# A chained attention, SwiGLU and bilinear kernel on one core: the second product in six groups of 768 tokens with streamed left factors

## The chip, the cores and the metric

One Trainium2 chip, one of its cores. The time is the device time of one execution in microseconds; the figure of a kernel is the median of its runs. The engines are TensorE (PE in the profile, its weight loads PEld), VectorE (DVE), ScalarE (ACT), GpSimd (POOL) and SyncE (SP), which issues most DMA transfers.

## What is computed

```python
p_packed = sm_attn(p, k, v)               # 8 batches, 8 heads, 576 tokens, 64 wide, 32 packed rows
out = sm_attn(q, p_packed, p_packed)
x = out.transpose(0, 2, 1, 3).reshape(4608, 512)
h = x @ w_in;  x = (h * sigmoid(h)) @ w_out          # 512 -> 2048 -> 512
a = x @ w1;    b = x @ w2                            # 512 -> 1024, twice
result = ((a * b) @ w3) @ w_out2                     # 1024 -> 1024 -> 512
```

All values are float32. The kernel holds each factor of a matrix product as a high and a low part and adds three products (high x high, low x high, high x low).

## The kernel before

The kernel has two stages. The first does the attention and the SwiGLU block ("first product": tiles `ps_h` and `ps_x`, matmuls of 288 columns) and writes its result x transposed to DRAM (`x2_d`), half a batch at a time, from a tile `xs`. The second ("second product") computes `a`, `b`, `a * b` and the output; `w3 @ w_out2` has been multiplied beforehand into `w34`.

The second product goes over 9 groups of 512 tokens and, in each, over 4 pairs `mp` of 128-wide blocks of the 1024 inner columns: 36 items, each one call of `emit_ab`. An item multiplies 2x2 blocks with seven products where eight would be needed (Winograd's form). Its left factors (seven per pair, made of `w1`, x = 0, and of `w2`, x = 1, at line 941) lie split in SBUF tiles `w`; its right factors are seven combinations of four quarters of the group's x (`x2r`), made by `right_factors` on VectorE (sums) and on ScalarE and VectorE (high and low part) into tiles `xcb..` and `xct..`. The seven products are matmuls of 256 columns (`product`, line 1236, here "y matmuls"); both x lie side by side in one of four PSUM banks `b1` to `b4`, 12 matmuls to a product. ScalarE and VectorE combine the banks (`p1`, `p5`, `r1`, `r2`; the copies at line 82, the additions at line 1257), VectorE multiplies a by b (`gate`, line 1260) and splits the result (`abh`, `abl`, lines 82 and 91). `emit_o` multiplies that by `w34`: 24 matmuls of 512 columns (lines 98 to 100, tile `ps_o`), added up over the four items of a group in four PSUM banks, which `evict` then copies and stores.

The left factors of pairs 0 and 1 come split from DRAM (`w12_d`, two loads of 1792 KB each); those of pairs 2 and 3 are made during the first two items by `last_left_factors` (sums on VectorE, high part on ScalarE, low part on GpSimd, line 91) straight into the tile `w12_23`. After that all left factors stay in SBUF.

The program is written as one order of instructions; a scheduler lays out each engine's queue at compile time by a model of times: of the instructions that it takes to be ready, the earliest in the program goes first. On the chip each queue then runs strictly in that order. Tiles of a pool opened later lie where earlier tiles lay, and wait until those are given up.

## Time and profile before

| | before |
|---|---|
| runs: median (lowest to highest) | 1437.81 us (1437.04 to 1439.02), 3 runs |
| profiled execution, span from first to last instruction | 1436.1 us |
| TensorE, VectorE, ScalarE, GpSimd busy | 97%, 63%, 47%, 42% |
| first y matmul of the second product | 862.2 us |
| last matmul | 1432.0 us |

A row of the profile names the line, the engine, the operation, the tile written and the tiles read, the shape, and how many. TensorE's durations overlap, since matmuls are pipelined: a spacing is taken from starts. A figure in square brackets is the idle time of the engine before the instruction and what ended it.

### The profile page before, as it was taken

How to read it: one execution, taken by the hardware profiler on the slowest of the kernel's cores; microseconds unless marked ns; L12 is line 12 of the kernel's file. 1: busy time of each engine (PE TensorE's matmuls, PEld its weight loads, DVE VectorE, ACT ScalarE, POOL GpSimd, SP SyncE). 2: the span in 40 equal slices, each digit the busy share in tenths (PEclk: the TensorE clock that was granted, in tenths of full speed). 3: DMA queues.
4: the chain of work that ended last, by engine and by line, in shares of the span. 5: the costliest groups of instructions: out<-in, count | busy, mean ns of one | idle time of the engine just before them, and what ended most of it. 6: DMA issues, size and time to landing. Idle time of an engine off the chain costs nothing.

```text
span 1436.1 us, 25890 instructions
## 1 busy us (share of the span) xinstructions
PE 1390.7 (97%) x9548; PEld 1308.4 (91%) x9548; DVE 901.6 (63%) x1687; ACT 672.2 (47%) x1474; POOL 605.5 (42%) x626
## 2 busy tenths in 40 slices
PE   7799899999999999999999999999999999999998
PEld 5578899899999999999998998999999999999998
DVE  5897756558766488666578855635454553645453
ACT  6866556655666555664556544323232231322221
POOL 2778755856779657687567534100000000000000
PEclk9999899999999999999999999999999999999999
DMA  8697544844568343563557667011010110101000
GB/s 319 198 308 253 163 150 142 265 152 146 170 184 249 123 155 121 170 190 116 178 162 252 204 228 298 23 38 46 15 60 1 60 29 31 59 2 60 1 30 30
DMA packets 135967, 193.07 MB, mean 134 GB/s; under 512 B 14496, under 2 KB 92576, under 8 KB 135328
## 3 DMA queue, kind: packets, MB, share of 16 engines
q1 hardware_dynamic: 125344, 178.82, 39.1%
q10 hardware_dynamic: 10496, 12.59, 2.5%
q8 instruction: 75, 1.23, 0.4%
q14 instruction: 52, 0.43, 0.1%
HBM read 132.38 MB, written 58.98 MB: 133 GB/s over the span
## 4 chain that ended last, share of the span: by engine, by line
PE 70%; DVE 9%; DMA 7%; issue 4%; POOL 4%; ACT 4%; SPq 2%; ACTq 0%; DVEq 0%; POOLq 0%
PE ps_ab L1236 24%; PE ps_x L100 6%; PE ps_x L98 6%; PE ps_x L99 6%; PE ps_o L98 5%; PE ps_o L99 5%; PE ps_o L100 5%; PE ps_h L98 3%; PE ps_h L100 3%; PE ps_h L99 3%; SPq L115 2%; DMA mr<-m_d 1%; DMA m_d<-ms 1%; POOL z L189 1%; DVE sbd L251 1%
## 5 line engine op out<-in xcount | busy, mean ns | idle before, releaser
L98 PE MATMUL ps_x<-gh,wo 128*128 128x288 f32 x1024 | 301.9, 298 | 2.7 <-ACT gh L82 1.2
L99 PE MATMUL ps_x<-gh,wo 128*128 128x288 f32 x1024 | 301.0, 296 | 0.0
L100 PE MATMUL ps_x<-gl,wo 128*128 128x288 f32 x1024 | 289.1, 297 | 1.9 <-POOL gl L91 1.6
L91 POOL TENSOR_TENSOR gl<-gg,gh 128x288 fp32r<-128x288 f32 x256 | 227.9, 893 | 101.5 <-ACT gh L82 82.5
L1236 PE MATMUL ps_ab<-xct,w 128*128 128x256 f32 x1728 | 223.0, 284 | 1.7 <-DVE r L1257 1.4
L1236 PEld LDWEIGHTS ps_ab<-xct,w 128*128 128x128 f32 x1728 | 215.6, 190 | 3.0 <-DVE r L1257 1.6
L98 PEld LDWEIGHTS ps_x<-gh,wo 128*128 128x128 f32 x1024 | 193.0, 189 | 6.1 <-DVE xs L883 2.0
L99 PEld LDWEIGHTS ps_x<-gh,wo 128*128 128x128 f32 x1024 | 193.2, 189 | 2.1 <-issue 1.2
L100 PEld LDWEIGHTS ps_x<-gl,wo 128*128 128x128 f32 x1024 | 188.1, 189 | 4.3 <-POOL gl L91 3.6
L82 ACT ACTIVATE gh<-gg 128x288 fp32r<-128x288 f32 x256 | 112.8, 443 | 165.8 <-DVE gg L846 158.2
L91 POOL TENSOR_TENSOR mq<-mr,mq 128x256 fp32r<-128x256 f32 x168 | 136.7, 814 | 109.0 <-DVE mq L86 54.4
L846 DVE SCALAR_TENSOR_TENSOR gg<-sg,ps_h 128x288 f32<-128x288 f32 x256 | 114.6, 448 | 107.3 <-ACT sg L841 55.3
L1236 PE MATMUL ps_ab<-xcb,w 128*128 128x256 f32 x1296 | 177.5, 283 | 0.7 <-ACT w L82 0.4
L98 PE MATMUL ps_h<-a,mq 128*128 128x288 f32 x512 | 155.9, 305 | 18.0 <-DVE gg L846 13.8
L1236 PEld LDWEIGHTS ps_ab<-xcb,w 128*128 128x128 f32 x1296 | 168.1, 189 | 5.6 <-ACT w L82 0.6
L1257 DVE TENSOR_TENSOR r<-p,ps_ab 128x512 f32<-128x512 f32 x72 | 49.2, 683 | 184.3 <-PE ps_ab L1236 184.1
L99 PE MATMUL ps_h<-a,mq 128*128 128x288 f32 x512 | 152.4, 298 | 0.0
L100 PE MATMUL ps_h<-a,mq 128*128 128x288 f32 x512 | 151.9, 297 | 0.0
L841 ACT ACTIVATE sg<-ps_h 128x288 f32<-128x288 f32 x256 | 103.4, 404 | 82.3 <-PE ps_h L100 48.6
L98 PEld LDWEIGHTS ps_h<-a,mq 128*128 128x128 f32 x512 | 96.7, 189 | 25.9 <-DVE gg L846 19.0
L82 ACT ACTIVATE p<-ps_ab 128x512 f32<-128x512 f32 x72 | 43.1, 598 | 146.2 <-PE ps_ab L1236 139.8
L100 PE MATMUL ps_o<-w,abh 128*128 128x512 f32 x280 | 109.5, 391 | 0.0
(172 smaller groups left out, 2645.3 us busy)
## 6 DMA issues: line engine op xcount, KB each, us to landing
mr<-m_d SPq DMA_DIRECT2D x144, 128.0 KB, 2.6
raw<-in_moe_w_dram SPq DMA_DIRECT2D x32, 512.0 KB, 4.4
wz<-wi_d SPq DMA_DIRECT2D x48, 256.0 KB, 3.8
m_d<-ms SPq DMA_DIRECT2D x96, 128.0 KB, 3.0
x_d<-xs SPq DMA_DIRECT2D x20, 576.0 KB, 3.4
raw<-in_moe_w_out_dram SPq DMA_DIRECT2D x22, 512.0 KB, 4.3
out_dram<-ob SPq DMA_DIRECT2D x36, 256.0 KB, 2.0
vr<-in_v_dram SPq DMA_DIRECT2D x14, 640.0 KB, 4.1
```

What stands on the lines that cost most here:

```text
L82: A.activation(out=dst, in_=src, func=ACTF.Copy, scale=mul)
L91: (eng or V).tensor_tensor(out=lo, in0=src, in1=hi.bitcast(F32), op=ALU.subtract)
L98: T.matmul(out=dst, lhsT=wh, rhs=xh, start=start, stop=False)
L99: T.matmul(out=dst, lhsT=wl, rhs=xh, start=False, stop=False)
L100: return T.matmul(out=dst, lhsT=wh, rhs=xl, start=False, stop=stop)
L115: return eng.dma_start(out=out, in_=in_)
L189: G.tensor_tensor(out=z, in0=z, in1=word(I32, 0), op=ALU.add)
L251: (act_copy if plain else V.tensor_copy)(dst[r, 0, :, r], src[r])
L841: ins = A.activation(out=sg, in_=ps, func=ACTF.Tanh, scale=0.5)
L846: ins = V.scalar_tensor_tensor(out=gg, in0=sg, scalar=1.0, in1=ps, op0=ALU.add, op1=ALU.mult)
L1236: T.matmul(out=bank[:, x], lhsT=w[:, wp], rhs=xt[:, kt, xp], start=first and (x, kt, n) == (0, 0, 0), stop=last and (x, kt, n) == (1, 1, 2 ...
L1257: V.tensor_tensor(out=dst, in0=p, in1=q, op=op)
```

## The change

The second product goes over 6 groups of 768 tokens. A quarter of the group's x is 384 columns wide, and the y matmuls have 384 columns. An item runs the seven products for x = 0 (`w1`) and then for x = 1 (`w2`), 6 matmuls to a product; the gates of both blocks are spread over the second half. The left factors are streamed: `load_unit` brings those of one pair and one x (1792 KB) into one of four buffers, as often as there are half-items, 48 times. Those of pairs 2 and 3 are now stored to `w12_d` when they are made, in the first items, and loaded again. Output sums go over one item in PSUM and over the four items of a group in SBUF tiles `oacc`, by a copy on ScalarE in the first item and an addition on VectorE in the others. For all groups but the first, the sums of the right factors are made on GpSimd (`right_sums`), and four of the seven low parts too. `load_x2` of the next group is queued behind the last store of `xs`. The order of the products and of `emit_o` within an item is as before.

```diff
-    w12_d = dram.tile([128, 2, 2, 2, 7, 2, 128], F32, name="w12_d")
+    w12_d = dram.tile([128, KM2 // 2, 2, 2, 7, 2, 128], F32, name="w12_d")
...
-            move(out=x2_d[b, f], in_=xs)
+            behind["xs"] = move(out=x2_d[b, f], in_=xs).ins
...
-                    store(out=w12_d[:, :, x, kt, j], in_=t, age=0)
+                    store(out=w12_d[:, 0:2, x, kt, j], in_=t, age=0)
...
-    NG = NT // 512
-    x2r, x2c, w12, w34 = {}, {}, {}, {}
+    W = 384
+    GT = 2 * W
+    NG = NT // GT
+    MP = KM2 // 2
+    assert NG * GT == NT
+    x2r, x2c, w34 = {}, {}, {}
+    RIGHT = ("b11", "t1", "t2", "t4", "b21", "t3", "b22")
+    LEFT = {name: j for j, name in enumerate(("a11", "a12", "a22", "s1", "s2", "s3", "s4"))}
...
+    def quarters(g):
+        return [x2r[g][:, 2 * i:2 * i + 2, W * j:W * j + W] for i in range(2) for j in range(2)]
+    def temp(pool, tag, bufs):
+        return pool.tile([128, 2, W], F32, tag=tag, name=tag, bufs=bufs)
+    def right_part(g, name, src, eng=None):
+        c = early.tile([128, 2, 2, W], F32R, tag=f"xc{name}", name=f"xc{name}")
+        split(c[:, :, 0], c[:, :, 1], src, eng=eng)
+        x2c[g][name] = c
...
+    def first_right_factors():
+        b11, b12, b21, b22 = quarters(0)
+        t = temp(early, "xt", 1)
+        x2c[0] = {}
+        minus(t, b12, b11)
+        minus(b12, b22, b12)
+        right_part(0, "b11", b11)
+        yield
+        right_part(0, "t1", t)
...
+    def right_sums(g):
+        b11, b12, b21, b22 = quarters(g)
+        t1, t2, t4 = temp(early, "xt", 1), temp(mid, "tmp", 2), temp(mid, "tmp", 2)
+        minus(t1, b12, b11, G)
+        yield
+        minus(b12, b22, b12, G)
+        yield
+        minus(t2, b22, t1, G)
+        yield
+        minus(t4, t2, b21, G)
+        sums_of[g] = dict(b11=b11, t1=t1, t2=t2, t4=t4, b21=b21, t3=b12, b22=b22)
     def right_factors(g):
-        r = x2r.pop(g)
-        b11, b12, b21, b22 = (r[:, 2 * i:2 * i + 2, 256 * j:256 * j + 256] for i in range(2) for j in range(2))
-        t = early.tile([128, 2, 256], F32, tag="xt", name="xt")
         x2c[g] = {}
...
-        part("b11", b11)
-        yield
-        part("t1", t)
...
+        for n, name in enumerate(RIGHT):
+            right_part(g, name, sums_of[g][name], V if n % 2 else G)
+            yield
+    wunits, came2 = [], []
+    def load_unit():
+        n = len(came2)
+        mp, x = divmod(n % (2 * MP), 2)
+        t = wunits[n % len(wunits)]
+        move(out=t, in_=w12_d[:, mp, x])
+        came2.append(t)
+    def room_unit(pool):
+        wunits.append(pool.tile([128, 2, 7, 2, 128], F32R, name=f"unit{len(wunits)}"))
...
     def last_left_factors():
+        def load(n):
+            t = low.tile([128, 2, 512], F32, tag="zl", name="zl", bufs=2)
+            for y in range(2):
+                move(out=t[:, y], in_=late_d[2 * n + y])
+            return [t[:, y] for y in range(2)]
+        z = load(0)
         for n in range(4):
             x, kt = divmod(n, 2)
-            sums = early.tile([128, 4, 256], F32, tag="sums", name="sums")
+            sums = low.tile([128, 4, 256], F32, tag="suml", name="suml")
             def part(j, src):
-                t = w12[2, 3][:, :, x, kt, j]
+                t = low.tile([128, 2, 2, 128], F32R, tag="w12s", name="w12s", bufs=7)
                 split(t[:, :, 0], t[:, :, 1], src.rearrange("p (j n) -> p j n", j=2), eng=G)
-            for step in left_factors([z12h.pop((n, y)) for y in range(2)], sums, part):
+                move(out=w12_d[:, 2:4, x, kt, j], in_=t)
+            nz = load(n + 1) if n < 3 else None
+            for step in left_factors(z, sums, part):
                 step()
+                left_steps[0] += 1
                 yield
-            if n < 2:
-                load_z12(n + 2)
+            z = nz
...
-            room_second(0, early)
-            load_second(0)
-            for n in range(2):
-                load_z12(n)
-            drain(right_factors(0))
+            for _ in range(2):
+                room_unit(early)
+                load_unit()
+            load_w34(early, 0)
+            drain(first_right_factors())
...
+    for _ in range(2):
+        room_unit(top)
+        load_unit()
     for mp in range(1, MP):
-        room_second(mp, wb, top if mp == 1 else None)
-    for mp in range(1, MP):
-        load_second(mp)
+        load_w34(mid, mp)
...
-    def product(bank, mp, g, left, right, first, last):
+    def product(bank, w, g, left, right, first, last):
         xt = x2c[g][right]
-        for x in range(2):
-            for kt in range(2):
-                w = w12[mp][:, x, kt, LEFT[left]]
-                for n, (wp, xp) in enumerate(((0, 0), (1, 0), (0, 1))):
-                    T.matmul(
-                        out=bank[:, x], lhsT=w[:, wp], rhs=xt[:, kt, xp],
-                        start=first and (x, kt, n) == (0, 0, 0), stop=last and (x, kt, n) == (1, 1, 2),
-                        skip_group_check=True,
-                    )
-    last_left = last_left_factors()
+        for kt in range(2):
+            for n, (wp, xp) in enumerate(((0, 0), (1, 0), (0, 1))):
+                T.matmul(
+                    out=bank, lhsT=w[:, kt, LEFT[left], wp], rhs=xt[:, kt, xp],
+                    start=first and (kt, n) == (0, 0), stop=last and (kt, n) == (1, 2),
+                    skip_group_check=True,
+                )
...
+        gated = {}
+        def gate(m, t):
+            r = [gated[x, m][:, t] for x in range(2)]
+            V.tensor_tensor(out=r[0], in0=r[0], in1=r[1], op=ALU.mult)
+            split(*(a[:, t * W:t * W + W] for a in abt[g, m]), r[0])
+        for x in range(2):
+            wt = came2[2 * i + x]
+            nxt = side[0]
+            if x and mp == MP - 1 and g + 1 < NG:
+                nxt = right_factors(g + 1)
+            steps = 3 if i < 2 else 1
+            def step():
+                for _ in range(steps):
+                    next(nxt, None)
+            b1, b2, b3, b4 = (ps_ab.tile([128, 512], F32, tag=f"ab{j}", name=f"ps_ab{j}")[:, 0:W] for j in range(4))
+            r1, r2 = room(f"r{x}0"), room(f"r{x}1")
+            gated[x, m1], gated[x, m2] = r1, r2
+            p1, p5 = (low.tile([128, W], F32, tag=f"p{j}", name=f"p{j}") for j in (1, 5))
+            product(b1, wt, g, "a11", "b11", True, False)
+            act_copy(p1, b1)
+            step()
+            product(b3, wt, g, "s1", "t1", True, False)
+            act_copy(p5, b3)
+            step()
+            product(b2, wt, g, "s2", "t2", True, False)
+            add(r1[:, 1], p1, b2)
+            step()
+            product(b4, wt, g, "a22", "t4", True, True)
+            step()
+            if i and not x and not final:
+                emit_o(i - 1)
+            product(b1, wt, g, "a12", "b21", False, True)
+            act_copy(r1[:, 0], b1)
+            if x:
+                room_ab()
+                gate(m1, 0)
+            step()
+            product(b2, wt, g, "s3", "t3", False, True)
+            add(r2[:, 1], p1, b2)
+            add(r2[:, 0], r2[:, 1], b4, ALU.subtract)
+            add(r2[:, 1], r2[:, 1], p5)
+            if x:
+                gate(m2, 0)
+            step()
+            product(b3, wt, g, "s4", "b22", False, True)
+            add(r1[:, 1], r1[:, 1], b3)
+            if x:
+                gate(m1, 1)
+                gate(m2, 1)
+            step()
+            while len(came2) < min(2 * len(items2), 2 * i + x + 1 + len(wunits)):
+                if left_steps[0] < {4: 22, 5: 44}.get(len(came2), 0):
+                    break
+                load_unit()
...
     def emit_o(i):
         g, mp = items2[i]
-        if mp == 0:
-            oacc[g] = [ps_o.tile([128, DM], F32, tag="o", name="ps_o") for _ in range(4)]
-        for m in reversed(pair(mp)):
-            h_, l_ = abt.pop((g, m))
-            for t in range(4):
-                ts = slice(128 * t, 128 * t + 128)
-                mm3(
-                    oacc[g][t], h_[:, ts], l_[:, ts], w34[m][:, 0], w34[m][:, 1],
-                    m == pair(0)[1], m == pair(MP - 1)[0],
-                )
-    def evict(i, t0):
-        g, mp = items2[i]
-        if mp < MP - 1:
-            return
-        for t in (t0, t0 + 1):
-            if i + 1 < len(items2):
-                ob = wb.tile([128, DM], F32, tag="ob", name="ob", bufs=2)
+        ab = {m: abt.pop((g, m)) for m in pair(mp)}
+        for t in range(GT // 128):
+            ts = slice(128 * t, 128 * t + 128)
+            ps = ps_o.tile([128, DM], F32, tag="o", name="ps_o")
+            for n, m in enumerate(pair(mp)):
+                h_, l_ = ab[m]
+                mm3(ps, h_[:, ts], l_[:, ts], w34[m][:, 0], w34[m][:, 1], n == 0, n == 1)
+            if mp == 0:
+                oacc[t] = mid.tile([128, DM], F32, tag=f"o{t}", name="ob")
+                act_copy(oacc[t], ps)
             else:
-                ob = early.tile([128, DM], F32, tag=("r0", "r1", "p1", "p5")[t], name="ob")
-            if t % 2:
-                V.tensor_copy(out=ob, in_=oacc[g][t])
-            else:
-                act_copy(ob, oacc[g][t])
-            r = 512 * g + 128 * t
-            DMA.dma_start(out=out[r:r + 128], in_=ob)
+                V.tensor_tensor(out=oacc[t], in0=oacc[t], in1=ps, op=ALU.add)
+            if mp == MP - 1:
+                r = GT * g + 128 * t
+                DMA.dma_start(out=out[r:r + 128], in_=oacc[t])
...
     for i, (g, mp) in enumerate(items2):
-        if i == 2:
-            drain(last_left)
+        if mp == 2 and g == 0:
+            drain(side[0])
+        if mp == 2 and g + 1 < NG:
+            side[0] = right_sums(g + 1)
+        if mp == 3 and g + 1 < NG:
+            drain(side[0])
         emit_ab(i)
         if mp == 0 and g + 1 < NG:
-            load_x2(g + 1)
+            with tc.issue_after(behind["xs"]):
+                load_x2(g + 1)
```

## Rows read from the trace of the kernel before

**Rows 1.** The page, part 1: busy time, share of the span, instructions.

```profile
span 1436.1 us, 25890 instructions
PE 1390.7 (97%) x9548; PEld 1308.4 (91%) x9548; DVE 901.6 (63%) x1687; ACT 672.2 (47%) x1474; POOL 605.5 (42%) x626
```

**Rows 2.** Busy time by window: PE, PEld, DVE, ACT, POOL, clock, DMA, GB/s.

```profile
1100.00:1200.00 100.00, 100.00 (x702) 93.97 (x701) 54.89 (x87) 30.64 (x52) 0.00 (x0) 1.00 0.13 43
```

**Rows 3.** Timeline of TensorE, second product: start, us, instruction, count.

```profile
1097.86 3.04 PE L1236 MATMUL ps_ab<-xcb,w 128*128 128x256 f32 x24
1100.74 4.48 PE L1236 MATMUL ps_ab<-xct,w 128*128 128x256 f32 x36
...
1105.54 1.08 PE L98 MATMUL ps_o<-w,abh 128*128 128x512 f32 x4
1106.46 0.77 PE L1236 MATMUL ps_ab<-xcb,w 128*128 128x256 f32 x5
1107.07 0.39 PE L99 MATMUL ps_o<-w,abl 128*128 128x512 f32 x1
...
1111.61 0.54 PE L1236 MATMUL ps_ab<-xcb,w 128*128 128x256 f32 x3
```

**Rows 4.** Timeline of TensorE, first product.

```profile
699.77 0.29 PE L98 MATMUL ps_x<-gh,wo 128*128 128x288 f32 x1
...
702.96 0.29 PE L98 MATMUL ps_x<-gh,wo 128*128 128x288 f32 x1
```

**Rows 5.** Timeline of TensorE, first items of the second product.

```profile
865.10 0.87 PE L1236 MATMUL ps_ab<-xcb,w 128*128 128x256 f32 x6
...
896.20 4.42 PE L1236 MATMUL ps_ab<-xct,w 128*128 128x256 f32 x19 [1.41 <-DVE r L1257]
...
912.24 4.49 PE L1236 MATMUL ps_ab<-xct,w 128*128 128x256 f32 x36
...
921.84 1.09 PE L98 MATMUL ps_o<-w,abh 128*128 128x512 f32 x4
```

**Rows 6.** Busy time by window, first items.

```profile
865.00:870.00 5.00, 5.00 (x43) 5.00 (x43) 2.96 (x7) 1.68 (x4) 0.00 (x0) 1.00 1.03 431
895.00:900.00 5.00, 3.81 (x18) 3.81 (x19) 4.38 (x6) 1.87 (x5) 5.00 (x6) 0.50 0.00 0
```

**Rows 7.** DMA issues: out<-in, queue, count, KB each, median us to landing.

```profile
w_d<-w12s ACTq DMA_DIRECT2D x28, 256.0 KB, 3.5
w<-w_d SPq DMA_DIRECT2D x4, 1792.0 KB, 13.8
```

**Rows 8.** Timelines of ScalarE and GpSimd: left factors of pairs 2 and 3.

```profile
879.80 1.03 ACT L82 ACTIVATE w<-z 128x256 fp32r<-128x256 f32 x3 [0.68 <-DMA x_d<-xs]
...
880.30 2.13 POOL L91 TENSOR_TENSOR w<-z,w 128x256 fp32r<-128x256 f32 x3 [16.79 <-ACT w L82]
...
905.05 2.13 POOL L91 TENSOR_TENSOR w<-sums,w 128x256 fp32r<-128x256 f32 x3 [1.45 <-ACT w L82]
```

**Rows 9.** Groups by line and shape, whole span: count, busy us, mean ns, idle before.

```profile
L91 DVE TENSOR_TENSOR e<-ps_t,e 128x384 fp32r<-128x384 f32 x12 | 6.7, 554 | 5.8 <-ACT e L82 5.8
L82 ACT ACTIVATE v<-vr 128x768 fp32r<-128x768 f32 x12 | 10.1, 841 | 8.5 <-PE ps_o L99 6.9 <-DMA wz<-wi_d 1.6
L91 POOL TENSOR_TENSOR v<-vr,v 128x768 fp32r<-128x768 f32 x12 | 22.3, 1857 | 3.9 <-ACT v L82 3.9
```

**Rows 10.** Timeline of VectorE, end of a steady item.

```profile
1098.06 0.69 DVE L1257 TENSOR_TENSOR r<-p,ps_ab 128x512 f32<-128x512 f32 x1 [9.58 <-PE ps_ab L1236]
1098.78 1.48 DVE L1257 TENSOR_TENSOR r<-r,ps_ab 128x512 f32<-128x512 f32 x2
...
1100.78 1.29 DVE L1260 TENSOR_TENSOR r<-r 128x512 f32<-128x512 f32 x2
```

**Rows 11.** Timeline of VectorE: GpSimd idle (second row), GpSimd working (the others).

```profile
502.64 1.76 DVE L251 CAST sbd<-pkT 32x64 fp32r<-32x64 f32 x1
...
865.67 0.42 DVE L941 TENSOR_TENSOR sums<-z 128x256 f32<-128x256 f32 x1
...
889.96 0.95 DVE L941 TENSOR_TENSOR sums<-z,sums 128x256 f32<-128x256 f32 x1
```

More of the change, by code (lines that the diff above doesn't have):

```diff
@@ new lines, in temp, with minus @@
+    def temp(pool, tag, bufs):
[4 more added lines that the diff above has]
+        x2c[g][name] = c
+    def minus(dst, p, q, eng=None):
+        (eng or V).tensor_tensor(out=dst, in0=p, in1=q, op=ALU.subtract)
+    def first_right_factors():
[7 more added lines that the diff above has]
+        right_part(0, "t1", t)
+        minus(t, b22, t)
+        yield
+        right_part(0, "t2", t)
+        minus(t, t, b21)
+        yield
+        right_part(0, "t4", t)
+        yield
+        right_part(0, "b21", b21)
+        yield
+        right_part(0, "t3", b12)
+        yield
+        right_part(0, "b22", b22)
+        yield
@@ L1097, in right_factors @@
-        t = early.tile([128, 2, 256], F32, tag="xt", name="xt")
         x2c[g] = {}
-        def part(j, src):
-            c = early.tile([128, 2, 2, 256], F32R, tag=f"xc{j}", name=f"xc{j}")
-            split(c[:, :, 0], c[:, :, 1], src)
-            x2c[g][j] = c
-        def add(dst, p, q):
-            V.tensor_tensor(out=dst, in0=p, in1=q, op=ALU.subtract)
-        add(t, b12, b11)
-        add(b12, b22, b12)
-        part("b11", b11)
-        yield
-        part("t1", t)
-        add(t, b22, t)
@@ L1114, in right_factors @@
[L1114 to L1133 removed]
+        for n, name in enumerate(RIGHT):
+            right_part(g, name, sums_of[g][name], V if n % 2 else G)
+            yield
@@ L1134, in room_second, with load_w34 @@
+    wunits, came2 = [], []
[7 more added lines that the diff above has]
+        wunits.append(pool.tile([128, 2, 7, 2, 128], F32R, name=f"unit{len(wunits)}"))
+    def load_w34(pool, mp):
         for m in pair(mp):
             w34[m] = pool.tile([128, 2, 512], F32R, name=f"w34_{m}")
-    def load_second(mp):
-        for x in range(2) if mp < 2 else ():
-            move(out=w12[mp][:, x], in_=w12_d[:, mp, x])
-        for m in pair(mp):
@@ L1242, in attention_swiglu_chain @@
[L1242 removed]
+        for kt in range(2):
[5 more added lines that the diff above has]
+                )
+    side = [last_left_factors()]
     def emit_ab(i):
         g, mp = items2[i]
[L1246 to L1254 removed]
+        final = i == len(items2) - 1
+        m1, m2 = pair(mp)
@@ L1270, in emit_ab @@
-        m1, m2 = pair(mp)
-        final = i == len(items2) - 1
-        spare = (("b11", "t1"), ("t2", "t4"))
-        product(b1, mp, g, "a11", "b11", True, False)
-        act_copy(p1, b1)
-        next(nxt, None)
-        product(b3, mp, g, "s1", "t1", True, False)
-        act_copy(p5, b3)
-        next(nxt, None)
-        product(b2, mp, g, "s2", "t2", True, False)
-        add(r1[:, :, 1], p1, b2)
-        next(nxt, None)
-        product(b4, mp, g, "a22", "t4", True, True)
-        next(nxt, None)
@@ L1284, in emit_ab, with room @@
-        if i and not final:
-            emit_o(i - 1)
-            evict(i - 1, 0)
-        product(b1, mp, g, "a12", "b21", False, True)
-        act_copy(r1[:, :, 0], b1)
-        next(nxt, None)
-        product(b2, mp, g, "s3", "t3", False, True)
-        add(r2[:, :, 1], p1, b2)
-        add(r2[:, :, 0], r2[:, :, 1], b4, ALU.subtract)
-        next(nxt, None)
-        product(b3, mp, g, "s4", "b22", False, True)
+        def room(tag):
+            return low.tile([128, 2, W], F32, tag=tag, name="r")
```

78 lines of the change are left out of this document (20 added, 58 removed).

## The prediction

> **What bounds the kernel now.** I read the page's busy shares first: over the whole span TensorE is busy 97% and VectorE 63% [rows 1], so only what shortens or interrupts TensorE's queue can move the end. Then one window of the second product: TensorE is busy 100.00 of 100 us, VectorE 54.89, ScalarE 30.64, GpSimd nothing [rows 2]. In the steady part no wait ends last; the queue is full, and the time is the number of matmuls times their spacing.
>
> The spacing comes from starts in TensorE's timeline, not from durations, which overlap. Twenty-four y matmuls of 256 columns start at 1097.86 and the next group at 1100.74: 2.88/24 = 120.0 ns. Twenty matmuls of 512 columns lie between 1107.07 and 1111.61: 4.54/20 = 227.0 ns [rows 3]. So a column costs (227.0 - 120.0)/256 = 0.418 ns and each matmul a fixed 13 ns. The 288-column matmuls of the first product test the line: 24 starts from 699.77 to 702.96, or 132.9 ns [rows 4]; the line says 133.4. A 384-column matmul lies half-way, at 173.5 ns.
>
> The second product has 36 items (9 groups of 512 tokens, 4 pairs of inner blocks), each of 84 y matmuls and 24 output matmuls. Its first stretch is not full. Ten y matmuls start before 865.10, 252 (three items) before 912.24, and the 48 output matmuls between them end before that (the 49th starts at 921.84) [rows 5]. Work: 242 x 0.120 + 48 x 0.227 = 39.9 us; elapsed: 47.1 us. So 7.2 us are lost there, among them 1.41 us of waiting for VectorE [rows 5] and a stretch in which TensorE, after several short waits, was granted 0.50 of its clock, the 1.2 GHz level [rows 6].
>
> **The matmuls.** y matmuls go from 3024 x 256 to 2016 x 384 columns: the same 774,144 columns, 1008 fewer fixed parts. 362.9 us become 349.8, or 13.1 us less; all of it is on the path, because TensorE is. The 864 output matmuls of 512 columns stay. The Trainium skill speaks against this: TensorE: Matmul & The Clock Gate, section Back-to-back issue gap, gives N/2.4 + 2.5 ns as the isolated spacing, by which the same edit would save only 1008 x 2.5 ns = 2.5 us. The rows show a fixed part five times as large, and they decide.
>
> **Loads of the left factors.** Each of the 48 half-items reads a unit of 1.8 MB; before, all of them stayed in SBUF. A full queue moved 431 GB/s [rows 6], so a unit takes 4.3 us, against a use of 42 x 0.1735 = 7.3 us plus on average 18 output matmuls, 4.1 us. Four buffers give a load two or three units of lead. In the steady part this hides: cost 0. Without that cover (a load behind a late one on SP's queue) it would cost a unit's 4.3 us once.
>
> **The first items.** The left factors of pairs 2 and 3 are now split by ScalarE and GpSimd, stored, and loaded again. Before, ScalarE waited at 879.80 for a store of xs, and only then could GpSimd begin [rows 8], because those factors lay where xs had lain; the change puts them elsewhere and sends the next group's load behind the xs store on SP's queue, which should start them some 3 to 7 us earlier. The need moves back as well: item 2 begins after two items of 84 x 0.1735 and one set of 36 output matmuls, 862 + 2 + 29.2 + 8.2 = 901, where before it was 889. Half of 26.9 us of GpSimd work [first and last of rows 8], a store of 3.5 us and a load of 4.3 to 13.8 us [rows 7] follow 875 to 880, so the unit lands between 896 and 911. Bounds of the stalls here: 0 to 13 us (10 of waiting and 3 at the lower clock); I take 3.5, half of today's 7.2, since most of the range lies before the need. Gain 3.7.
>
> **VectorE's tail at each half-item.** Banks b1 to b4 now turn over in one 1.04 us product where it was 1.44. The nearest row for an operation on 384 columns from PSUM is 554 ns [rows 9]. Today VectorE follows the last products with add, subtract and add, then two gating multiplies [rows 10], and the release of b3 is ready in time. In the change the first gates stand ahead of the add that frees b3. From the end of x=1's sixth product: add 0.55, subtract 1.1, add 1.6, multiply 2.1, add that frees b3 2.7 us; TensorE wants b3 at 1.9. So 0.8 us late in the order of the code. But the order on TensorE follows a model of readiness: four output matmuls with the high part are pulled ahead of those with the low part, and five y matmuls between them [rows 3]. Bank b2 is free at 0.6 us, so the third product can pass the second. Bounds 0 to 1.2 us per item; I take 1 us in all, nearer to today's rows, where nothing waits.
>
> **Group edges.** Four of seven low parts of the right factors, and all four sums, move from VectorE to GpSimd, per edge (five edges). A GpSimd operation on 768 elements takes 1857 ns, the high part on ScalarE 841 [rows 9]. VectorE's `tensor_tensor` with both inputs in SBUF does not run beside it: `sums` takes 0.42 us while GpSimd is idle and 0.95 us while it works, and a 32x64 cast waited 1.76 us beside 768- and 512-element operations [rows 11]. The Trainium skill says why: SBUF — State Buffer, section SBUF: two separate sides, makes the shared port pair an exclusive lock for a whole instruction. These traces agree.
>
> Walked through the last half-item of a group (its first matmul at 0, products every 1.04): GpSimd's b11 from 2.7 to 4.5; VectorE's t1 till 5.3; GpSimd's t2 till 7.0; VectorE's t4 till 7.8; GpSimd's b21 till 9.5; the first gate till 10.0; only then the add that frees b2, at 10.5. Without the lock it comes at 7.5. The next item's first product ends at 8.3, so TensorE can stand 2.2 us, or 0.6 to 1.1 if another product or the b21 product is ahead in its queue. Bounds per edge: 0 (all passed by) to 5 (b3 and the gates late as well). I take 1.5, and 0.4 for the four sums, which fall beside the gates of the group's first item: 5 x 1.9 = 9.5 us.
>
> **Elsewhere.** Output sums: six adds of 512 columns per item run beside 8.2 us of output matmuls with four banks, cost 0. VectorE's work per item comes to 18 x 0.55 + 6 x 0.69 = 14 us [rows 9, 10] of 22.7. The end keeps its shape: last matmul, one VectorE operation on 512 columns, one store. The first right factors are 1.5 times as long on VectorE but begin 10 us before the first y product: 0 to 1 us, taken in the 3.5 above.
>
> **Sum.** On the profiled execution's 1436.1 us: -13.1 - 3.7 + 1 + 9.5 = -6.3, so 1429.8; the median of the runs stands 1.7 us above that span: **1431.5 us**.
>
> **The rivals.** (a) *Clean edges.* TensorE's order passes every late bank and the first items lose little: 1437.8 - 13.1 - 1 to - 7, so 1417.5 to 1424. For it: no TensorE wait from 915 on today. Against it: the lock.
> (b) *Slower: VectorE's tail becomes the bound.* Place: the boundary between x=1 and the next x=0. Price: 1.2 us x 23 = 27.6, so about 1459 with the forecast's other terms. It decides from the point where the second product stays right behind the first in TensorE's queue while b3's add stands behind the gates. For it: 1.04 us of cover instead of 1.44. Against it: VectorE has 45% idle now, and order follows readiness. Half of that price gives 1445.
> (c) *Late units.* Pairs 2 and 3 arrive at the late bound, 10 us, and TensorE then runs at its lower level for a stretch, 3 us: 1431.5 - 3.5 + 13 = 1441. For it: the queue at 431 GB/s around 865 [rows 6].
> (d) *The fixed part doesn't fall* with the number of matmuls but by the 2.5 ns of the page named above: 10.6 us are missing, 1442. The three sizes on one line speak against it.
>
> **How the numbers follow.** Forecast 0.46, (a) 0.22, (b) 0.18, (c) 0.11, (d) 0.03. What a measurement here can tell is about 0.2%, 2.9 us. The forecast's own bounds (edges 0 to 5 us, start 0 to 13) run from about 1422 to 1446; three quarters of its chance lies below 1434.9. Faster: 0.36 + 0.22 = 0.58; same: 0.07 + parts of (b), (c), (d) 0.11 = 0.18; slower: 0.24. The range runs from the low end of (a), 1418, to 1446, which holds the forecast's bounds, (c), (d) and the mild half of (b).
>
> **What would show it.** Spacing of the 384-column starts: 173.5 ns; if not, (d). TensorE's waits by line: entries "ps_ab <- DVE r" of 1 to 2 us, five times, 90 us apart, mean the edges; 23 times, (b); none, (a). "PE <- DMA" near 900 to 917 means (c). Long VectorE durations (over 1 us for 384 columns) beside GpSimd's 768-element rows mean the lock. The forecast is wrong if TensorE's order passes the late banks, or if the scheduler's order leaves them where the code does.

## The result and the profile after

| | before | after |
|---|---|---|
| median (lowest to highest) | 1437.42 us (1435.31 to 1439.02) | 1458.14 us (1457.74 to 1458.90) |
| profiled execution, span | 1436.1 us | 1455.7 us |
| first y matmul | 862.2 us | 864.7 us |
| last matmul | 1432.0 us | 1451.6 us |

The ratio is 1.0144, with a 95% interval of 1.013 to 1.0159: the change made the kernel 20.7 us slower. The forecast was 1431.5 us, in a range up to 1446, so both the sign and the range were wrong.

The busy shares of the page after the change answer [rows 1]:

```profile
span 1455.7 us, 24332 instructions
PE 1388.5 (95%) x8540; PEld 1298.9 (89%) x8540; DVE 959.4 (66%) x1812; ACT 685.3 (47%) x1531; POOL 684.9 (47%) x666
```

TensorE is busy 2.2 us less, in a span 19.6 us longer: it now waits. What for is in its waits by line (total us, times, longest), first the longest of the kernel before from 865 us on, then those of the changed kernel:

```profile
PE ps_ab L1236 <- DVE r L1257: 1.4, 1, 1.4
```

```profile
PE ps_h L98 <- DVE gg L846: 16.2, 14, 3.8
PE ps_ab L1272 <- DMA unit<-w_d: 16.1, 2, 11.3
...
PE ps_ab L1272 <- DVE r L1286: 4.0, 5, 0.8
```

The first line is of the first stage, where the kernel before stood 13.8 us in 16 waits. Two waits for a unit of left factors make 16.1 us. Five waits for VectorE are the group edges, one each. Where the two lie is in TensorE's timeline, which answers [rows 5]:

```profile
903.16 1.22 PE L1272 MATMUL ps_ab<-xct,unit 128*128 128x384 f32 x6
...
916.79 0.39 PE L100 MATMUL ps_o<-w,abh 128*128 128x512 f32 x1
922.02 2.29 PE L1272 MATMUL ps_ab<-xcb,unit 128*128 128x384 f32 x6 [4.84 <-DMA unit<-w_d]
...
943.12 2.26 PE L1272 MATMUL ps_ab<-xcb,unit 128*128 128x384 f32 x6 [11.27 <-DMA unit<-w_d]
945.18 4.36 PE L1272 MATMUL ps_ab<-xct,unit 128*128 128x384 f32 x18
...
952.50 1.23 PE L1272 MATMUL ps_ab<-xcb,unit 128*128 128x384 f32 x6
```

The second item's last y product starts at 903.16 and is over at 904.2. The third item, the first one of pair 2, starts at 922.02; the prediction had it at 901. In between TensorE does the output matmuls of the second item, up to 917.2. The third item's second half, x = 1, starts at 943.12. The windows (columns as in [rows 2]) tell what the chip did meanwhile:

```profile
920.00:925.00 5.00, 2.98 (x9) 2.98 (x10) 0.00 (x0) 0.91 (x2) 1.09 (x2) 0.52 1.05 419
...
935.00:940.00 5.00, 0.00 (x0) 0.00 (x0) 0.00 (x0) 0.00 (x0) 0.00 (x0) 0.50 1.00 427
...
1100.00:1200.00 100.00, 99.20 (x514) 91.80 (x513) 55.57 (x96) 30.15 (x58) 15.89 (x8) 1.00 0.50 179
```

From 935 to 940 every engine stands and the DMA queues are full: 427 GB/s. After each wait TensorE starts at 0.50 of its clock, the 1.2 GHz level, as in [rows 6]. In the steady part it is busy 99.20 of 100 us, where it was 100.00 [rows 2].

For the accounts I use one measure. *Lost* in a stretch is its length less the matmuls that start in it, each at its steady spacing: 120.1 ns for 256 columns, 132.9 for 288, 175.4 for 384, 229.3 (before) or 231.5 (after) for 512; each is a mean over the differences of starts in the steady part (of 288, in the first stage). From the first y matmul to the start of the fourth item 7.2 us were lost before and 25.3 after. Of the 25.3, 16.1 are the two waits for units, and some 4.7 the half clock behind them (an estimate: the 0.50 lasted 5.0 us from 922.02 on and 4.4 us from 943.12 on). The account of the 19.6 us:

- y matmuls: 3024 x 120.06 = 363.1 us became 2016 x 175.4 = 353.6: **-9.5**
- output matmuls: 864 x (231.5 - 229.3): **+1.9**
- first y matmul later: **+2.5**
- first items: 25.3 - 7.2: **+18.1**
- edges: a group takes 93.48 us and, without the edge wait (shown below), 92.24, five times: **+6.2**

That is +19.2; 0.4 us are not accounted for.

### The profile page after: what moved, and what is told of

Its sections match the earlier page's. It is cut to its first block, busy times and chain, and to the rows that moved or that the text cites. A ratio compares the mean times of both kernels' runs of the same rounds, so it can differ in the third digit from the quotient of the medians.

```text
span 1455.7 us, 24332 instructions
## 1 busy us (share of the span) xinstructions
PE 1388.5 (95%) x8540; PEld 1298.9 (89%) x8540; DVE 959.4 (66%) x1812; ACT 685.3 (47%) x1531; POOL 684.9 (47%) x666
## 4 chain that ended last, share of the span: by engine, by line
PE 72%; DVE 9%; DMA 7%; issue 5%; ACT 4%; POOL 2%; SPq 1%; ACTq 0%; DVEq 0%; POOLq 0%
PE ps_ab L1272 22%; PE ps_x L98 6%; PE ps_x L99 6%; PE ps_x L100 6%; PE ps_o L98 5%; PE ps_o L99 5%; PE ps_o L100 5%; PE ps_h L98 3%; PE ps_h L100 3%; PE ps_h L99 3%; DMA m_d<-ms 1%; DMA unit<-w_d 1%; DVE gg L846 1%; DMA mr<-m_d 1%; PE ps_w L98 1%
## 5 line engine op out<-in xcount | busy, mean ns | idle before, releaser
L1272 PE MATMUL ps_ab<-xct,unit 128*128 128x384 f32 x1152 | 231.1, 340 | 4.0 <-DVE r L1286 4.0
L1272 PEld LDWEIGHTS ps_ab<-xct,unit 128*128 128x128 f32 x1152 | 206.4, 190 | 9.7 <-DVE r L1286 6.6
L1272 PE MATMUL ps_ab<-xcb,unit 128*128 128x384 f32 x864 | 179.3, 340 | 16.1 <-DMA unit<-w_d 16.1
L91 POOL TENSOR_TENSOR xcb<-x2r,xcb 128x768 fp32r<-128x768 f32 x15 | 32.5, 2183 | 308.7 <-ACT xcb L82 308.7
L1272 PEld LDWEIGHTS ps_ab<-xcb,unit 128*128 128x128 f32 x864 | 155.6, 190 | 22.2 <-issue 11.8
L1286 DVE TENSOR_TENSOR r<-p,ps_ab 128x384 f32<-128x384 f32 x96 | 52.8, 550 | 129.7 <-PE ps_ab L1272 129.6
L82 ACT ACTIVATE p<-ps_ab 128x384 f32<-128x384 f32 x96 | 47.1, 492 | 176.0 <-PE ps_ab L1272 99.9
```

Of the source, the lines that this page charges most:

```text
L82: A.activation(out=dst, in_=src, func=ACTF.Copy, scale=mul)
L91: (eng or V).tensor_tensor(out=lo, in0=src, in1=hi.bitcast(F32), op=ALU.subtract)
L1272: T.matmul(out=bank, lhsT=w[:, kt, LEFT[left], wp], rhs=xt[:, kt, xp], start=first and (kt, n) == (0, 0), stop=last and (kt, n) == (1, 2), ...
L1286: V.tensor_tensor(out=dst, in0=p, in1=q, op=op)
```

## Where the units were held up

SyncE's queue in the stretch of the two waits (start, time to issue, transfer, how many):

```profile
914.65 0.37 SPq L115 DMA_DIRECT2D unit<-w_d  x1
915.07 0.44 SPq L115 DMA_DIRECT2D w_d<-w12s  x1
915.55 0.47 SPq L115 DMA_DIRECT2D unit<-w_d  x1
916.12 13.87 SPq L115 DMA_DIRECT2D w_d<-w12s  x8
931.88 2.15 SPq L115 DMA_DIRECT2D unit<-w_d  x3
```

The load at 914.65 is pair 2, x = 0, wanted first; the one at 915.55 is pair 3, x = 0, wanted two halves later. The eight stores behind it are the last left factors of x = 1. Of the three loads at the end, the first belongs to the next *group*, and only the second is pair 2, x = 1, for which TensorE stands: its last store landed at 933.0, it was issued at 933.1 and landed at 943.0. Issues between 840 and 960 (KB each, median us to landing) answer [rows 7]:

```profile
unit<-w_d SPq DMA_DIRECT2D x10, 1792.0 KB, 11.2
w_d<-w12s SPq DMA_DIRECT2D x28, 256.0 KB, 5.2
```

The stores themselves were late because the factors were made late. ScalarE (high parts) and GpSimd (low parts) answer [rows 8]:

```profile
879.51 1.02 ACT L82 ACTIVATE w12s<-zl 128x256 fp32r<-128x256 f32 x3
...
922.73 0.42 ACT L82 ACTIVATE w12s<-suml 128x256 fp32r<-128x256 f32 x1 [3.32 <-DMA w_d<-w12s]
...
928.37 0.42 ACT L82 ACTIVATE w12s<-suml 128x256 fp32r<-128x256 f32 x1 [1.61 <-DVE r L1286]
```

```profile
880.00 2.79 POOL L91 TENSOR_TENSOR w12s<-zl,w12s 128x256 fp32r<-128x256 f32 x3 [13.21 <-ACT w12s L82]
...
928.86 0.74 POOL L91 TENSOR_TENSOR w12s<-suml,w12s 128x256 fp32r<-128x256 f32 x1 [4.90 <-ACT w12s L82]
```

They begin at 880, as before, but end at 929.6 instead of 907.2. Two things held them up, one after the other. First ScalarE's own queue: in the new order copies of PSUM, for which TensorE had not finished, stand ahead of the high parts. The eighth high part came right behind such a copy:

```profile
891.75 0.60 ACT L82 ACTIVATE ob<-ps_o 128x512 f32<-128x512 f32 x1 [2.44 <-PE ps_o L100]
892.25 0.41 ACT L82 ACTIVATE w12s<-zl 128x256 fp32r<-128x256 f32 x1
```

It is the first that uses a `w12s` buffer again, and by the trace's landing times the store that had to empty this buffer was done at 885.0. Of ScalarE's 28.9 us of idle time between its first and its last high part, 10.9 ended with TensorE (2.2 of 12.3 before), 4.9 of these at `ob`, copies of output sums that the change has put on ScalarE. So the fourteenth low part, the last that pair 2, x = 0, needs, ended 28.2 us after the first began, with no wait for a buffer. Its store had landed by 911.1; the load stood behind five more stores in SyncE's queue until 914.65. Second, the buffers: only the last two high parts stood for one. They start at 922.73 and 928.37, within 0.11 us of the landings that freed their buffers (922.65 and 928.26, though the last row names VectorE), and these stores had been issued beside the two unit loads in a full DMA queue.

## The experiments

In all of them the lines of the kernel shift by a few; the names stay. Times are medians; where a ratio stands it is against the kernel before on the same chip. Where none stands the time is that of one run; ten runs of one kernel (three edits, below) lay between 1439.0 and 1443.2 us, so the trace's own account in the table further down is the firmer reading there.

**Without the late factors.** Pairs 2 and 3 read the units of pairs 0 and 1.

```diff
         mp, x = divmod(n % (2 * MP), 2)
+        mp %= 2
...
-    side = [last_left_factors()]
+    side = [iter(())]
```

> Leaves out the making, storing and reloading of the left factors of pairs 2 and 3; their units are read from those of pairs 0 and 1, so the output isn't the reference's. The pad keeps the places of the other tiles. Theory (the two waits for units, 5.0 and 11.4 us, and the lower clock around them are the loss): 16 to 20 us less than the changed kernel, 1438 to 1442, and at most 4 us lost before the fourth item. Rival (VectorE and ScalarE would have been late there anyway): at most 8 us less, 1450 or more, with waits for VectorE in the place of those for units. Under both the five waits of 0.96 us at group edges stay.

Measured: 1435.51 us, ratio 0.9975 (0.9966 to 0.9985). 1.2 us were lost up to the fourth item. Leaving out the late factors takes 22.6 us from the changed kernel, more than the 16 to 20 expected, and turns the sign. It is not all a cost of the change: the kernel before makes these factors too, with 7.2 us lost in its first items, and a kernel before without them was not run.

**Unit loads in order of use.**

```diff
-        move(out=t, in_=w12_d[:, mp, x])
+        with tc.issue_after(behind["unit"]) if "unit" in behind else ExitStack():
+            behind["unit"] = move(out=t, in_=w12_d[:, mp, x]).ins
```

> The unit loads are queued on SP in the order in which they are used, so that the load for the next group no longer goes ahead of the one that TensorE waits for at 931. Theory (that load takes 4.3 us of the queue): the 11.4 us wait becomes about 7, the time 1453 to 1455. Rival (the last stores of the left factors, landed at 933.0, set it): less than 1.5 us changes, 1456.5 to 1459.

Measured: 1448.66 us, so some 9.5 us of the 20.7 came from the order on SyncE's queue (9.4 by what was lost up to the fourth item), about twice what was expected. The waits for units fell to 8.7 us:

```profile
PE ps_ab L1273 <- DMA unit<-w_d: 8.7, 2, 5.6
```

**All low parts of the edges on VectorE.**

```diff
-            right_part(g, name, sums_of[g][name], V if n % 2 else G)
+            right_part(g, name, sums_of[g][name])
```

> All seven low parts of the right factors on VectorE, as before the change; the four sums stay on GpSimd. Theory (at group edges VectorE waits for the port while GpSimd's 768-element operations run): the five waits of 0.96 us go, 5 to 6 us less, 1452 to 1453. Rival (VectorE simply has too much to do there): four more operations of 0.95 us per edge, the waits grow to 2 to 4 us, 1463 to 1473.

Measured: 1451.35 us, 6.8 us less, of which five groups at 92.24 us instead of 93.48 make 6.2. VectorE got more work, and the waits for it went. One edge of the changed kernel shows why, on VectorE, GpSimd and TensorE:

```profile
1161.13 2.01 DVE L91 TENSOR_TENSOR xct<-tmp,xct 128x768 fp32r<-128x768 f32 x1 [0.51 <-ACT xct L82]
1163.06 0.54 DVE L1286 TENSOR_TENSOR r<-r,ps_ab 128x384 f32<-128x384 f32 x1
1163.53 1.73 DVE L1303 TENSOR_TENSOR r<-r 128x384 f32<-128x384 f32 x1
1165.18 0.54 DVE L1286 TENSOR_TENSOR r<-p,ps_ab 128x384 f32<-128x384 f32 x1
...
1167.74 0.95 DVE L91 TENSOR_TENSOR xct<-x2r,xct 128x768 fp32r<-128x768 f32 x1
```

```profile
1160.44 1.88 POOL L91 TENSOR_TENSOR xct<-tmp,xct 128x768 fp32r<-128x768 f32 x1 [0.82 <-ACT xct L82]
1162.28 4.66 POOL L91 TENSOR_TENSOR xcb<-x2r,xcb 128x768 fp32r<-128x768 f32 x2
```

```profile
1165.78 1.31 PE L1272 MATMUL ps_ab<-xct,unit 128*128 128x384 f32 x6 [0.80 <-DVE r L1286]
```

Beside GpSimd, VectorE's cast of 768 elements takes 2.01 us, where the same form takes 0.95 when GpSimd is done, and a multiply of 384 takes 1.73 (0.55 elsewhere in the steady part). The addition between them, which has an input in PSUM, keeps its 0.54. The addition behind them frees the bank for which TensorE stands. This is the lock on operations with both inputs in SBUF that [rows 11] showed and that the Trainium skill states (SBUF — State Buffer, section SBUF: two separate sides); the run agrees with it, at 1.24 us an edge. In the window that lost 0.8 us above, nothing is lost here:

```profile
1100.00:1200.00 100.00, 100.00 (x520) 92.87 (x519) 55.93 (x101) 31.44 (x60) 7.69 (x4) 1.00 0.50 179
```

**GpSimd's sums for the next group behind the last left factor.**

```diff
+        with tc.issue_after(behind["left"]):
+            minus(t1, b12, b11, G)
```

> GpSimd's four sums for group 1, 8.3 us between 888 and 900, are queued behind its last left factor. Theory (GpSimd's queue sets when the left factors are done): they end about 8 us earlier, the waits for units shrink by 8 us, 1449 to 1451. Rival (GpSimd mostly waits for ScalarE's high parts, and those for loads, buffers and VectorE): the last left factor moves by less than 3 us, 1455 to 1458.

Measured: 1458.61 us, no change; the last left factor came at 930.1 instead of 929.6. GpSimd's 8 us of sums are not what delays the factors: it waits for ScalarE.

**The late factors made at the end of the first stage.**

```diff
-    side = [last_left_factors()]
+    side = [iter(())]
...
+                    eng = G if half and j % 2 else V
+                    split(t[:, :, 0], t[:, :, 1], src.rearrange("p (j n) -> p j n", j=2), eng=eng)
+                    store(out=w12_d[:, 2 * half:2 * half + 2, x, kt, j], in_=t, age=0)
```

> The left factors of pairs 2 and 3 are made and stored at the end of the first stage, with those of pairs 0 and 1, instead of in the first items of the second product; half of the 28 low parts on GpSimd, half on VectorE. Theory (the loss is that these units come late, and ScalarE, VectorE and GpSimd have room in the first stage): near the 1435.5 us of the run without those factors, 1435 to 1441, no wait for a unit. Rival (the first stage has no room: TensorE waits there for VectorE and GpSimd): the first y product starts 8 us later or more, 1443 or more.

Measured: 1451.97 us, ratio 1.0096 (1.0079 to 1.0113). No unit is late, but the first y matmul starts at 876.5, 11.8 us later. The first stage has no room for the work: over half of the 18.1 us that the first items lost more than before appears again there.

**The buffers of the units changed over from the second group on.**

```diff
-        t = wunits[n % len(wunits)]
+        t = wunits[(n + 2 * (n >= 8)) % len(wunits)]
```

> From the second group on the units of pairs 0 and 2 lie in the two buffers that those of pairs 1 and 3 had, and the other way round. In the changed kernel the 384-column matmuls of pairs 0 and 2 are 174.3 ns apart, those of pairs 1 and 3 176.7. Theory (the place of the weights sets it): the two change roles. Rival (what runs beside those pairs sets it): pairs 1 and 3 stay at 176.7. One more wait for units at the switch is to be expected; the time itself says nothing, 1458 to 1475.

Measured: 1463.43 us. Two units of the first group are overwritten before they are read here, so part of its product is made with other factors. What counts is the spacing. First the changed kernel, pair 1 (first three lines) and pair 2 of the third group, then the same pair 1 with the buffers changed over:

```profile
1110.18 3.34 PE L1272 MATMUL ps_ab<-xct,unit 128*128 128x384 f32 x18
1113.36 2.28 PE L1272 MATMUL ps_ab<-xcb,unit 128*128 128x384 f32 x12
1115.48 1.23 PE L1272 MATMUL ps_ab<-xct,unit 128*128 128x384 f32 x6
...
1133.22 3.28 PE L1272 MATMUL ps_ab<-xct,unit 128*128 128x384 f32 x18
1136.34 1.89 PE L1272 MATMUL ps_ab<-xcb,unit 128*128 128x384 f32 x10
```

```profile
1115.83 3.28 PE L1272 MATMUL ps_ab<-xct,unit 128*128 128x384 f32 x18
1118.94 2.24 PE L1272 MATMUL ps_ab<-xcb,unit 128*128 128x384 f32 x12
1121.03 1.20 PE L1272 MATMUL ps_ab<-xct,unit 128*128 128x384 f32 x6
```

Thirty starts of pair 1 take 5.30 us (176.7 ns each), eighteen of pair 2 3.12 us (173.3); with the buffers changed over the thirty take 5.20 us (173.3). Over the whole steady part, pairs 0 to 3 stand at 174.5, 176.6, 174.0 and 176.6 ns, and changed over at 176.7, 174.6, 176.6 and 174.2. The spacing goes with the buffer in which the weights lie.

**Loads that nobody wants yet, moved behind the first half of the stores.**

```diff
+            with tc.issue_after(left_store[1, 6]):
+                for m in pair(2):
+                    move(out=w34[m], in_=w34_d[m])
+                load_x2(1)
+                for m in pair(3):
+                    move(out=w34[m], in_=w34_d[m])
```

> The loads of w34 of pairs 2 and 3 (2 MB) and of the second group's x (1.6 MB) are queued on SP behind the 14th store of the left factors. Theory (the left factors wait for free buffers, whose stores land late behind these loads in a full DMA queue): the 14th store lands 6 to 10 us earlier, the two waits for units shrink from 16.4 us together to 4 to 8, 1447 to 1451. Rival (the order in which ScalarE was given its work holds the high parts back, whatever the queue): less than 3 us, 1455 to 1458.

Measured: 1450.22 us, 7.9 us less. Of these, 4.7 were lost less up to the fourth item, and 2.8 are an earlier first y matmul (861.9), which varies as much among kernels that don't touch it. The first of the two waits is gone and the second has grown to 13.6; the load for the next group still went ahead, and with the order mended as well 6.6 are left (three edits, below):

```profile
PE ps_ab L1275 <- DMA unit<-w_d: 13.6, 1, 13.6
```

GpSimd was done with the factors at 919.8 instead of 929.6, with the same work on the same engines. That looks like the theory, in which buffers come free earlier, but the trace says otherwise. With the loads moved the scheduler also laid out ScalarE's queue anew: the eighth high part now stands ahead of the copies.

```profile
884.88 0.40 ACT L82 ACTIVATE w12s<-zl 128x256 fp32r<-128x256 f32 x1
885.99 0.49 ACT L82 ACTIVATE r<-ps_ab 128x384 f32<-128x384 f32 x1 [0.71 <-DVE abl L91]
```

ScalarE's idle time behind TensorE fell from 10.9 to 3.4 us, while its waits for a buffer rose from some 4.9 to 6.2. So the earlier end rests on what the rival named, ScalarE's order, though the rival expected no gain. Whether the scheduler chose the order because its model has the stores land late was not tried.

**The first group's right factors later in the program.**

```diff
+        if i == prep_end + 2:
+            drain(first_right_factors())
...
-            drain(first_right_factors())
```

> The first group's right factors are put into the program two items later, behind two more operations of the first product on VectorE. Theory (TensorE's wait of 2.8 us at 857 comes from VectorE standing at the first right factor, whose x has not landed, with the gate of the first product behind it): that wait falls under 0.8 us, the first y product starts 2 us earlier, 1455 to 1456.5. Rival (the time is lost anyway, since the second item waits for units): the first product starts earlier and the units' waits grow by the same, 1457.5 to 1458.5.

Measured: 1459.02 us. The scheduler left VectorE's queue as it was and the wait stayed (2.7 us), so this decides nothing.

**Three edits together** (order of the units, edges on VectorE, later loads).

> Three of the edits together: unit loads queued in order of use, all seven low parts of right factors on VectorE, and the loads of w34 of pairs 2 and 3 and of the second group's x2r behind the 14th store of left factors. If the delays lie one behind the other and are separate (queue order, edges, stores landing late), the three single gains add up, taken from the changed kernel's 1458.1: 9.5 + 6.8 + 7.9, which gives 1433.9, a little faster than the kernel before. Rival: two of them shorten the same wait for unit 5. With the later loads alone the last stores landed at 927.4, and unit 5 is wanted at 922.4; in the right order it would be issued at 927.4 and land 4.3 us later, 931.7 against 936.2, so order brings only 4.5 us there: 1450.2 - 4.5 - 6.8 = 1438.9, level with the kernel before.

Measured: 1441.17 us, ratio 1.0019 (1.0009 to 1.0029). The gains do not add up to the 1433.9 of the theory: order and later loads shorten the same waits, as the rival had it, though its 1438.9 was missed by 2.3 us too.

**Nine buffers for the stores.** To those three edits:

```diff
-name="w12s", bufs=7)
+name="w12s", bufs=9)
```

> The kernel of e9_combined with nine w12s buffers in place of seven. If ScalarE's waits for a free w12s buffer (4.5 us for one store at 915.8 with the later loads alone) set when the last left factor is made, two more buffers let it run two stores ahead, the last stores land some 4.5 us earlier and the wait for unit 5 falls by as much: 4.5 us under e9_combined. Rival: GpSimd's low parts, or ScalarE's copies of PSUM that stand between its high parts, set it; then the time is that of e9_combined within 1 us.

Measured: 1439.53 us, ratio 1.0006 (0.9995 to 1.0018). The median is 1.6 us lower, where 4.5 were expected, and the profiled spans are 1437.3 and 1437.2 us: little or no gain. The buffers did what they should, since GpSimd was done at 913.8 instead of 921.2, but the last store landed at 925.9 instead of 924.5. What is left stands on SyncE's queue:

```profile
897.29 1.56 SPq L115 DMA_DIRECT2D w<-w_d  x2
...
907.16 1.18 SPq L115 DMA_DIRECT2D w<-w_d  x1
...
911.14 0.33 SPq L115 DMA_DIRECT2D unit<-w_d  x1
```

The moved loads have only come to lie between the stores of the second half and ahead of the unit, which is issued at 911.1 and lands at 921.1.

**Neither late factors nor edge waits**: the first and the third experiment together.

> The kernel of e1_no_late (it leaves out making, storing and loading the left factors of pairs 2 and 3, and reads the units of pairs 0 and 1 in their place) with all seven low parts on VectorE. It is what the new shape costs with neither late factors nor edge waits. The edges took 6.8 us in the whole change; if they are independent of the late factors, 1435.5 - 6.8 = 1428.7. Rival: VectorE, without the waits for the units, becomes the bound beside the fourth pair, because it has seven casts of 0.95 to 1.76 us more per group; then less than half of it comes back, 1432 or above.

Measured: 1427.00 us, ratio 0.9919 (0.9901 to 0.9936). This is what the new shape gives without its two side effects: 11.4 us under the kernel before. The spacing makes 7.6 of them (9.5 - 1.9); 5.2 are lost less in the first items (2.0 for 7.2), because work that the kernel before does is left out here; the first y matmul comes 1.1 later.

**The queue in order of need.** Edges on VectorE, nine buffers, units in order of use, every late load in its place, and four steps of left factors at a time in the first item where there were three:

```diff
+        if n == 4:
+            behind["unit4"] = behind["unit"]
+        if 4 <= n < 8:
+            with tc.issue_after(behind["unit"]):
+                if n == 6:
+                    load_x2(1)
+                else:
+                    for m in pair({4: 1, 5: 2, 7: 3}[n]):
+                        behind["unit"] = move(out=w34[m], in_=w34_d[m]).ins
...
-                move(out=w12_d[:, 2:4, x, kt, j], in_=t)
+                with tc.issue_after(behind["unit4"]) if "unit4" in behind else ExitStack():
+                    move(out=w12_d[:, 2:4, x, kt, j], in_=t)
...
-            steps = 3 if i < 2 else 1
+            steps = (4, 3)[i] if i < 2 else 1
```

> The edits of e10_more_rooms except its place for the later loads: here w34 of pair 1 is loaded behind unit 4, w34 of pair 2 behind unit 5, the second group's x2r behind unit 6, w34 of pair 3 behind unit 7, the stores of left factors that come after unit 4's load wait behind it on SP's queue, and the first item emits four steps of left factors for three, so that unit 4's load is 18 stores back and not 21. In e10_more_rooms 3.5 MB of loads that nobody wants before 930 stood between the stores, unit 4's load was issued at 911.1 and took 10 us to land, at 921.1, where a unit alone takes 4.3 us. If the crowd on the DMA queues is the cause that is left, unit 4 is issued near 901 and lands near 906 (wanted at 904), the last stores land near 916 and unit 5 near 921 (wanted at 917): some 6 us of waits beside 1427.0 without late factors, 1433 to 1435, faster than the kernel before by 0.2 to 0.4%. Rival: the left factors are made no faster than 1 us each behind ScalarE's other work and unit 5's wait only takes over what unit 4's loses: 1438 to 1440, as e10_more_rooms.

Measured: 1433.57 us, ratio 0.9966 (0.9954 to 0.9978): faster than both kernels, by 0.3% against the kernel before. By the account, -9.5 + 1.9 for the matmuls, +1.6 for the start and +0.6 for the first items make -5.4, and the profiled spans differ by 5.2. The edits were not tried one by one, so what the queue and what the four steps gave stays open. TensorE's only wait for a unit, and SyncE's queue:

```profile
PE ps_ab L1287 <- DMA unit<-w_d: 2.6, 1, 2.6
```

```profile
900.26 0.55 SPq L115 DMA_DIRECT2D unit<-w_d  x1
900.87 1.20 SPq L115 DMA_DIRECT2D w<-w_d  x2
...
919.45 0.33 SPq L115 DMA_DIRECT2D unit<-w_d  x1
```

The load of pair 2, x = 0, is issued 14.4 us earlier than in the changed kernel, at 900.26. The accounts side by side (lost: from the first y matmul to the fourth item; period: one steady group, for the kernel before 768 tokens):

| | first y | lost | period | median |
|---|---|---|---|---|
| before | 862.2 | 7.2 | 93.5 | 1437.4 |
| after | 864.7 | 25.3 | 93.48 | 1458.1 |
| late factors left out | 863.2 | 1.2 | 93.47 | 1435.5 |
| units in order | 864.9 | 15.9 | 93.48 | 1448.7 |
| edges on VectorE | 865.5 | 24.4 | 92.24 | 1451.4 |
| loads later | 861.9 | 20.6 | 93.48 | 1450.2 |
| three edits | 864.1 | 13.6 | 92.24 | 1441.2 |
| no late factors, edges on VectorE | 863.3 | 2.0 | 92.24 | 1427.0 |
| queue in order of need | 863.8 | 7.8 | 92.24 | 1433.6 |

## Why the prediction was wrong, point by point

**The first items: the step that failed.** It put the unit's landing between 896 and 911 and the need at 901, and took 3.5 us of stalls, with a bound of 13, for a gain of 3.7. The need came at 904.2, close to the forecast; the unit landed at 921.98. In all 25.3 us were lost, past the bound, or 18.1 more than before. Three things in it were wrong.
- It took half of today's 26.9 us of GpSimd work, 13.4, as the time to the last store of x = 0. Measured were 28.2 us, and 49.6 for all 28 low parts. GpSimd's work [rows 8] was paced by ScalarE, and the prediction kept the pace of the old queue for a new one. In the new queue the high parts stand behind copies for which TensorE had not finished, among them the copies of the output sums, which *Elsewhere* left out when it put the output sums at 0. It also costed the stores' latency at the end of the chain and not what a late store does to a later factor; this link showed in the last two factors only.
- It looked at one unit. The second half of pair 2 has a unit of its own, and its wait was the longer one, 11.27 us.
- It left the queue out. "Without that cover (a load behind a late one on SP's queue) it would cost a unit's 4.3 us once" stood in *Loads of the left factors*, at a cost of 0. That case came, and in order of use some 9.5 us came back. The rule to walk a queue past each moved instruction was kept for VectorE and not for SyncE and ScalarE, whose orders the scheduler chose anew.

**The matmuls.** Forecast -13.1, measured -9.5 and, for the output matmuls taken as unchanged, +1.9. The straight line through three sizes gave 173.5 ns, and two of the four buffers run at 174.0 to 174.5; the others at 176.6 to 176.7, which no row of before could show. The 512-column spacing was read from one stretch of 20 matmuls at 227.0 [rows 3], where the mean before was 229.3. The fixed part does fall with the number of matmuls, so rival (d) is out. By an estimate from N/2.4 + 2.5 ns (the Trainium skill, TensorE: Matmul & The Clock Gate, section Back-to-back issue gap) the y matmuls would have saved 2.5 us; the runs show 9.5. Why the output matmuls stand 2.2 ns further apart was not tried.

**VectorE's tail** was right: there is no such wait outside the five edges (forecast +1, measured 0), and TensorE's order is not that of the code. In the rows of the third group above, eighteen matmuls with `xct` are followed by twelve with `xcb` and only then by six with `xct`: the product with b22, into b3, has gone ahead of the one with t3. That this order is what spares the wait is argued, not tried. Rival (b) named a time of 1459, next to the measured one, and yet its mechanism did not happen; the five entries "ps_ab <- DVE r" where it wanted 23 say so.

**Group edges.** The mechanism was right, lock and all, and the size too large: 1.9 us an edge forecast, 1.24 measured, 0.80 of it as one wait.

**Elsewhere.** The first right factors were to cost 0 to 1 us, "10 us before the first y product". The first y matmul came 2.5 us later. In the changed kernel VectorE stands 4.70 us for `x2r`, and its products for the first stage (`gg`) queue behind the sums and low parts:

```profile
855.62 0.96 DVE L1111 TENSOR_TENSOR xt<-x2r 128x768 f32<-128x768 f32 x1 [4.70 <-DMA x2r<-x_d]
856.50 1.82 DVE L91 TENSOR_TENSOR xcb<-x2r,xcb 128x768 fp32r<-128x768 f32 x2
...
859.97 0.44 DVE L846 SCALAR_TENSOR_TENSOR gg<-sg,ps_h 128x288 f32<-128x288 f32 x1
```

The one run meant to test this did not move it, so the cause is argued and not shown. The start also varies from 861.9 to 867.8 among kernels that don't touch this place (the highest with the buffers of the units changed over), so 2.5 us is within what it varies by itself.

**Rival (c)**, late units with the lower clock behind, is what happened. It had a chance of 0.11 and a price of 13 because I held the late bound of one unit for the worst case. From the forecast's -6.3 to the account's +19.2, it is 21.8 us for the first items (18.1 + 3.7), 5.5 for the matmuls, 2.5 for the start, less 3.3 for the edges and 1 for the tail.

## What to carry to other kernels

When work is turned from "written in place" to "stored and loaded again", walk the whole ring: buffer, store, queue, load and the next use of the buffer; a full DMA queue can slow the maker as well as the reader. Look also at what the maker's own queue now puts ahead of the work: here copies that wait for TensorE held up the first half of the factors, and no buffer did. List every load on the issuing queue in order of need and tie that order down, since a scheduler that orders by its own model may put a load for the next round ahead of the one that is waited for. A gain in the steady part (here 7.6 us) is small beside one disturbed start, so price the start first.

## What the runs showed of the hardware

The spacing of matmuls depends on the place of the weights in SBUF: 174.0 to 174.6 ns for 384 columns with the weights in one pair of buffers and 176.6 to 176.7 in the other, and it changed over with the buffers. It did not depend on the traffic: in the changed kernel the mean was 175.2 ns in stretches with a DMA share over 0.8 and 175.5 in those under 0.1. What it is in the two places that differs was not tried. The 256-column matmuls before stood at 120.0 ns throughout.
